# Attention with two dense layers on one core: the second layer's products 1, 5 and 2 run over gate pairs 0 to 3 before pairs 4 to 7, with a new list of places

## The chip, the cores and the metric

The kernel runs on one core of a Trainium2 chip, as one launch. The metric is the device time of that launch in microseconds. Engines are named as the profile names them: PE (matmul) with PEld (its weight loads), DVE (vector), ACT (scalar), POOL (GpSimd) and SP, which issues all DMAs here. Each engine takes its instructions in the order in which they stand in the program and waits on semaphores for the others.

## The reference

```python
def _attn_ref(q, k, v):                        # (4, 8, 576, 64) each
    ...                                        # pooled attention: means over 4 neighbours, 144 x 144, softmax
    out_up = np.repeat(out_d, 4, axis=2)
    mask = np.abs(pos[:, None] - pos[None, :]) < 4
    ...                                        # banded attention over the same q, k, v
    return out_up + out_local

x = attention, as (2304, 512)
h = x @ moe_w_in                               # (512, 2048)
x = (h / (1 + exp(-h))) @ moe_w_out            # (2048, 512)
h = x @ moe2_w_in
out = (h / (1 + exp(-1.702 * h))) @ moe2_w_out
```

The four weight matrices are float64.

## The kernel before

**Steps and places.** The kernel does not issue its work while it computes it. It adds 2663 steps to a plan (`add(name, engine, duration, function, reads, writes, buffers)`), and a string, `PLACES`, holds two characters for each step: its place in the program. `placed` reads them, checks them against the graph of dependencies, and the steps are issued in that order. So each engine's order is a table of numbers. A second table, `ON`, names the steps that run on another engine than the usual one.

**Start.** The float64 weights arrive as pairs of 32-bit words and are rebuilt in steps `ca`, `cz`, `sg`, `cs`, `cp` (ACT, DVE or POOL), then split into a high and a low fp16 half by `hi` (ACT, L376) and `lo` (DVE, L380). Each fp32 matmul of the layers is three fp16 matmuls over these halves (`TERMS`). The attention of 32 units (4 batches, 2 halves of the sequence, 4 pairs of heads) runs beside that and, from the second batch on, beside the first layer. A unit u is, in short: `KT`/`QT` (PE transposes), `SC` scores (PE), `LC`, `DM`, `LS`, `LU`, `RC`, `LN`, `PT` (DVE or POOL), `DE`, `LE`, `DN`, `TC` (ACT, some on DVE), `TP` and `AV` (PE), `UC` (ACT, L1292), `XA` (DVE, L1300). The bank that `KT` of one pair of heads writes is free again when `XA` of an earlier unit has read it.

**First layer.** Eight blocks of 288 tokens; each has 8 pairs of 128-column tiles: `h1.m.p` (PE, L702), tanh (ACT, L714), `g0` (DVE, L717), `gh` (ACT, L724), `gl` (DVE, L727), then `o1.m` (PE, L819, for block 0 L847). The PE's order among these is fixed by `chain`.

**Second layer.** Nine blocks of 256 tokens. `h_pair2(n, p)` makes gate pair p of block n: 24 matmuls into a PSUM tile (PE, L881), `th` (ACT, L893), `g0` (DVE, L896), `gs`, three additions that form the sums of Strassen's scheme (L900 to L902, on DVE or POOL as `ON` says), `gh` (ACT, L906), `gl` (DVE, L909). After the 8 pairs, `block2(n)` runs seven products of 24 matmuls each (L960) over the pairs, three matmuls per pair, into three PSUM banks `oy`, `ox` and `oz`. Of a pair's three matmuls the first two read the high half of the gate (made by `gh`), the third the low half (made by `gl`). `PARTS` lists the pieces (product, first pair, end) in PE's order:

```python
PARTS = ((1, 0, 4), (1, 4, 7), (5, 0, 4), (5, 4, 7), (2, 0, 4), (1, 7, 8), (5, 7, 8), (2, 4, 6), (6, 0, 4), ...
for prod, p0, p1 in PARTS:
    ...
    gk = [f"g{bk}.{p}" for p in range(p0, p1)]
    s = add(f"o{bk}.{prod}.{p0}", "PE", mm(3 * (p1 - p0), D2), f, r=wk + gk + [(x, "l") for x in gk], w=[bank[acc]], ...)
    chain(s)
```

Banks are read out by `e` (ACT L938, DVE L944) between products that share one. `dx`, `rm`, `am`, `pw`, `xh`, `xl` make the scales and fp16 halves of a later block's input; the PE's part of it is two matmuls (`rm`, L771).

Of the kernel before, what the change touches and what calls it, by code (L numbers as in the profile page):

```python
# [42 lines left out]


PLACES = (
    "0006020804070x030A1C0V1d2b1k050d111o2e010j0h0w0m0L0T090y1a0J1f0P1r0b0Z0M1315181l0c0U12101m1c20171L1N1P1V1U2c1I2g2r2m2y2s2C2j2M2Q2Y2Z30"
# [3 lines left out]
    "2l2x2B2p2F2I2K2L2O2R2S2W353d3n3h444w66828A2n1X2V3S2P2U2X37313c383b3k3m3u3r3v3K3H3O3X4041333f3j3y3t3D3z3J3L3P3T42464d4n4v4C4N5K43474b4i"  # L50
    "4m4o4r4y4B4H4O4R545g5h5m5w5z5C4Q4X505b5c5i5k5o5q5s5y5x5F5H5E5L5U5W5X63656A6Z768sai2G3E6148324u7s4U527B8b6f7d8o6r5R3Q3V4j5f5l5Y6n6b6s6o"
    "6x6z6B6H6F6J6T6P7e7n7t9k494c5B5N5Q6D6X6L776Y7l7v7C7M7J7N7Z7W81878c8z5T6g8j6V7w7z7P7L7U8d8f8m8n8u8r8x8H8F8K8Q8T927S7Y8O7p7x8h8B8l8D8q8v"
    "8I8L8N8R8W908X9497989b9p9u9y9Cac9FeM72858J9v8G939a9h9f9l9i9o9G9J9O9K9S9Wa9abafalbM8V8Z9w9Q9N9Z9R9Va3a5a8a7aqaCaNaOaTb1bV9maoasaAavaKaz"
    "aQaSaUaWb0b5bcaXbvbGbKbOaxaEb3b6bjb9brbtbwbybAbCbPbRbNbUbXbYbZc3c9cbchcPeoja6Q9Eag9n7XcCd3aMaFcYe9bLbxdmcHboaDbnbEb4bic0c6c5cac7cccfcg"
    "cjcmcDcOcxcVd7d9fCbqcucUbebgcycFcIcKcNcQcTcXdId6djdldLdQdUdXe3bscMdfcwczdgdqdudHdvdKdNe4e5eaedele7eCeGeIfscicldEcZd2e6egerenevexezeAeB"
    "eEeLePeDeTeXeZf0fJfNfPfTg8hXm5dceue0fbdAdCf1f4f6f9fafdfefgflfqfwfzfofYg5gcgZf8fufvfBfEfGfHfMfSfUfVfZgggjgmgEh0h3jhg0g3gfghgqgzgwgBgGgN"
    "h6gPhHhKhxhWi2i5i8gTgXh8hkhihMhmhnhPhThZi9ieihibikiuiwiMjujyjAjPjRkMjEdsfhg6gdejifgSh1gKjzitiXfRkGiWkHj4fFfKhoilioiyiDiEiLiIiJiQiRjliZ"
    "jijOk8kakgkhm1fxiVjrhrhvjejmjIjWjLjMk1k3k7ktkxkIkNl1lbldlehtjZkwj9jbkrkDkykOkPkWkYkZlWlmlwlAlYm6mdmemJl4lhlXkmkvlplGlslLlvlJlOlSlUm2mi"
    "mlmhmmmomqmLmNmVngnknMogrrjGkqlTlFkTkUmvmxmEmzmKmRmUn4njndnrnLnDnTo3odpRlulInnnsnynNnEnVnXokoqonozoKotoRoYp5qln3o7ofowouoDoEoHoJoOp6oU"
    "papopeprpPpTq9oQoTp8pbpfpkpjpqpsptpVpFpXq0q8qbqfqhqiqmqsqtqvqGquqw393w3M3Y4E4J3F3W4a4f4l4T4k4A4K4P4V4Z4F4S5d5j5p5v575e5r5G5P685t5S646l"  # L60
    "6v7k6e6k6C6G898e6t6w6I6S7G7R6O6W7f71797o7i7r7A7E7I807O7V8i868a8t8k8p8C8y8E8M8P8Y95999c9L969d9q9t9x9A9j9r9z9D9Haa9B9I9P9T9Ya19M9Ua2a6ay"
# [24 lines left out]
)
# [1435 lines left out]
```

## Time and profile before

| | us |
|---|---|
| median of 3 runs | 902.23 (901.01 to 902.79) |
| the profiled execution: its time | 902.26 |
| the profiled execution: span from first to last instruction | 900.5 |
| PE busy | 864.3 (96%) |
| DVE busy | 623.0 (69%) |
| ACT busy | 464.0 (52%) |
| POOL busy | 150.3 (17%) |

The span divides into four stretches: to 68.2 us no matmul of a layer runs; to about 150 us the first block of the first layer runs while weights are still rebuilt; to 532.9 us the other seven blocks; from there the second layer. Busy time of PE is modelled and runs from one matmul's start to its end, so a wait between two matmuls shows as an idle time in brackets in the timeline, or as a later start.

### The profile page before, as it was taken

To read this page: it belongs to the slowest core of one execution; us is meant where nothing else is said; L and a number is where in the kernel's file an instruction comes from. 1 tells how busy PE (TensorE), PEld (TensorE's weight loads), DVE (VectorE), ACT (ScalarE), POOL (GpSimd) and SP (SyncE) were. 2 spreads that over 40 slices of the span, in tenths; PEclk is the share of its full clock that TensorE was granted. 3 is DMA by queue.
4 is the path that set the end of the run, shared out by engine and by line. 5 is a ranking of instruction groups with operands and counts; after the bars stand their busy time and mean duration, and the time that the engine had idled before them with its cause. 6 is when DMAs were issued, how large, how long until landed. Compare 5 with 4: busy or idle time off the path is not lost.

```text
span 900.5 us, 23832 instructions
## 1 busy us (share of the span) xinstructions
PE 864.3 (96%) x10212; PEld 717.7 (80%) x10212; DVE 623.0 (69%) x1365; ACT 464.0 (52%) x820; POOL 150.3 (17%) x165
## 2 busy tenths in 40 slices
...
GB/s 269 204 241 230 190 63 113 69 89 127 120 118 155 150 104 98 121 106 84 129 13 293 66 41 1 12 1 24 1 25 1 36 1 13 1 36 1 25 13 36
DMA packets 116190, 77.04 MB, mean 86 GB/s; under 512 B 94836, under 2 KB 101492, under 8 KB 115060
## 3 DMA queue, kind: packets, MB, share of 16 engines
...
## 4 chain that ended last, share of the span: by engine, by line
PE 66%; DVE 25%; ACT 4%; issue 2%; DMA 2%; SPq 0%; ACTq 0%; DVEq 0%
PE hps L702 18%; PE ops L819 16%; PE oy L960 8%; DVE g L909 7%; PE hps L881 6%; PE oz L960 4%; DVE tg L896 4%; DVE tg L901 2%; PE ox L960 2%; PE ops L847 2%; DVE tg L900 2%; PE ul L1286 2%; DVE tg L902 2%; PE sl L1204 2%; DMA kraw<-in_k_dram 1%
## 5 line engine op out<-in xcount | busy, mean ns | idle before, releaser
L702 PE MATMUL hps<-xhl,win 128*128 128x288 f16 x1536 | 197.9, 288 | 0.0
L881 PE MATMUL hps<-xhl,win 128*128 128x256 f16 x1728 | 191.0, 273 | 0.2 <-DVE tg L896 0.2
L881 PEld LDWEIGHTS <-win 128*128 128x128 f16 x1728 | 168.9, 98 | 20.5 <-issue 0.6
L702 PEld LDWEIGHTS <-win 128*128 128x128 f16 x1536 | 148.9, 99 | 37.8
L819 PE MATMUL ops<-g,wout 128*128 128x288 f16 x1344 | 170.8, 287 | 0.0
L960 PEld LDWEIGHTS <-g 128*128 128x128 f16 x1512 | 146.6, 98 | 25.5 <-DVE g L909 6.5
L819 PEld LDWEIGHTS <-wout 128*128 128x128 f16 x1344 | 129.8, 98 | 32.8 <-issue 0.6
L893 ACT ACTIVATE tg<-hps,blk 128x512 f32<-128x512 f32 x72 | 49.3, 685 | 136.9 <-PE hps L881 128.8
L896 DVE SCALAR_TENSOR_TENSOR tg<-tg,hps 128x512 f32<-128x512 f32 x72 | 49.1, 682 | 54.6 <-ACT tg L893 54.6
L906 ACT ACTIVATE g<-tg 128x896 f16<-128x896 f32 x72 | 67.6, 944 | 32.1 <-DVE tg L902 30.6
L909 DVE SCALAR_TENSOR_TENSOR g<-tg,g 128x896 f16<-128x896 f32 x72 | 78.3, 1094 | 7.5 <-ACT g L906 7.2
L960 PE MATMUL oy<-wout,g 128*128 128x256 f16 x648 | 75.1, 273 | 0.3 <-DVE o L944 0.3
L714 ACT ACTIVATE tg<-hps,blk 128x576 f32<-128x576 f32 x64 | 47.1, 737 | 45.7 <-PE hps L702 37.4
L900 POOL TENSOR_TENSOR tg<-tg 128x128 f32<-128x128 f32 x9 | 6.8, 755 | 368.9 <-DVE tg L896 368.9
L717 DVE SCALAR_TENSOR_TENSOR tg<-tg,hps 128x576 f32<-128x576 f32 x64 | 47.7, 746 | 27.4 <-ACT tg L714 27.0
L348 POOL TENSOR_TENSOR cs<-cs,cz 128x512 int32<-128x512 int32 x32 | 43.0, 1346 | 134.1 <-DVE cz L336 87.6
L727 DVE SCALAR_TENSOR_TENSOR g<-tg,gs,g 128x576 f16<-128x576 f32 x56 | 47.0, 847 | 6.4 <-ACT g L724 6.3
L724 ACT ACTIVATE g<-tg,gs 128x576 f16<-128x576 f32 x56 | 42.8, 769 | 15.8 <-DVE tg L717 15.7
L938 ACT ACTIVATE o<-oy,blk 128x256 f32<-128x256 f32 x27 | 12.7, 471 | 53.8 <-PE oy L960 53.8
L323 ACT ACTIVATE st<-st 128x512 f32<-128x512 f32 (+1 forms) x48 | 39.0, 824 | 1.2 <-DMA st<-in_moe_w_out_dram 0.8
L944 DVE SCALAR_TENSOR_TENSOR o<-oy,blk,o 128x256 f32<-128x256 f32 x9 | 4.4, 484 | 47.5 <-PE oy L960 24.4
L1234 ACT ACTIVATE pd<-sl,nm 72x144 f32<-72x144 f32 x64 | 23.4, 369 | 24.1 <-DVE sc L1219 11.8
...
## 6 DMA issues: line engine op xcount, KB each, us to landing
...
```

The lines of the kernel that those rows point to most:

```text
L348: eng.tensor_tensor(out=s, in0=s, in1=zget(), op=ALU.add)
L702: nc.tensor.matmul(o, T[w][:, kc, a, fc * P:(fc + 1) * P], T[xk][:, kc, b, :T_], start=(n == 0), stop=(n == 3 * KC - 1))
L714: ACT.activation(out=T[tg], in_=T[ps][:, :, :T_], func=AF.Tanh, scale=T["a" + bk][:, c:c + 1])
L717: DVE.scalar_tensor_tensor(out=T[tg], in0=T[tg], scalar=1.0, in1=T[ps][:, :, :T_], op0=ALU.add, op1=ALU.mult)
L727: DVE.scalar_tensor_tensor(out=T[g][:, 1], in0=T[tg], scalar=gs, in1=T[g][:, 0], op0=ALU.mult, op1=ALU.subtract)
L819: nc.tensor.matmul(o, w[:, j, a, dc * P:(dc + 1) * P], g[:, b, j % 2, :], start=(n == 0), stop=(n == 3 * NF - 1))
L881: nc.tensor.matmul(o, T[w][:, kc, a, fc * P:(fc + 1) * P], T[xk][:, kc, b, :], start=(n == 0), stop=(n == 3 * KC - 1))
L893: ACT.activation(out=four(), in_=T[ps][:, 0, :], func=AF.Tanh, scale=T["a" + bk][:, c:c + 1])
L896: DVE.scalar_tensor_tensor(out=four(), in0=four(), scalar=1.0, in1=T[ps][:, 0, :], op0=ALU.add, op1=ALU.mult)
L906: ACT.activation(out=T[g][:, 0], in_=T[tg], func=AF.Copy, scale=GS2)
L909: DVE.scalar_tensor_tensor(out=T[g][:, 1], in0=T[tg], scalar=GS2, in1=T[g][:, 0], op0=ALU.mult, op1=ALU.subtract)
L960: nc.tensor.matmul(T[bank[acc]], g[:, a, slot, :], w, start=first and p == p0 and i == 0, stop=prod in (2, 3, 4) and p == NF // 2 - 1 and ...
```

## The change

Two things change. In `PARTS`, the four pairs 0 to 3 of products 1, 5 and 2 come first, then pairs 4 to 6 of products 1 and 5, then pair 7 of both; the rest of the list stands. And `PLACES` and `ON` are others: every engine's order is a new one.

```diff
 ON = {
-    "POOL": ("cp1.in.0.2 cp1.in.3.2 cp1.out.0.0 cp1.out.1.0 cp1.out.1.2 cp1.out.2.0 cp1.out.2.2 cp1.out.3.0 cp1.out.3.2"),
-    "DVE": ("sg1.in.1.2 sg1.in.2.0 sg1.out.0.0 sg1.out.1.2 LN0 LS1 LS2 LN2 LS3 LN3 LS6 LS11 LS13 LN14 LN17 LS18 LN18 LS19 "
...
-    "ACT": ("DN0 DN1 DN2 DN3 DN5 DN6 DN7 DN8 DN9 DN10 DN11 DN13 DN16 DN23 DN26"),
+    "DVE": ("sg1.in.0.0 sg1.in.0.2 sg1.in.1.2 sg1.in.3.0 sg1.out.0.2 sg1.out.1.2 LS0 LN0 LS1 LN1 LN4 LN7 LN9 LN10 LS12 LN12 "
...
+    "POOL": ("cp1.out.0.0 cp1.out.0.2 cp1.out.1.0 cp1.out.1.2 cp1.out.2.0 cp1.out.2.2 cp1.out.3.0 cp1.out.3.2"),
+    "ACT": ("DN0 DN1 DN3 DN5 DN6 DN7 DN8 DN9 DN10 DN11 DN12 DN14 DN20 DN21 DN24 DN25 DN26 DN27 DN30"),
 }
...
 PLACES = (
-    "0006020804070x030A1C0V1d2b1k050d111o2e010j0h0w0m0L0T090y1a0J1f0P1r0b0Z0M1315181l0c0U12101m1c20171L1N1P1V1U2c1I2g2r2m2y2s2C2j2M2Q2Y2Z30"
+    "0006020403070q050U1j0z1a221n0i0j0Z1v27010x080K0B0N0Y090C0R0Q110S1k0c0X0T1510181u0b0M14131A1d1B171L1Q252y2l2C1s26292j2o2r2z2f2R332Y3b36"
...
-    PARTS = ((1, 0, 4), (1, 4, 7), (5, 0, 4), (5, 4, 7), (2, 0, 4), (1, 7, 8), (5, 7, 8), (2, 4, 6), (6, 0, 4), (6, 4, 8), (3, 0, 4), (3, 4, 8),
+    PARTS = ((1, 0, 4), (5, 0, 4), (2, 0, 4), (1, 4, 7), (5, 4, 7), (1, 7, 8), (5, 7, 8), (2, 4, 6), (6, 0, 4), (6, 4, 8), (3, 0, 4), (3, 4, 8),
```

The sums `gs` that run on POOL are nine before (block 0: pairs 0, 2, 5; block 3: pairs 0, 1, 3, 4; block 4: pair 0; block 8: pair 0) and thirteen now (block 0: 0, 2, 4; blocks 1, 2 and 5: pair 0; block 3: 3, 4; block 6: 1, 2, 3, 4, 6).

**PE, the products of block 5.** The first three pieces as they stood, one row for each change of pair that matters; the number behind `g` names the pair (10825 is pair 3, 10859 pair 4, 10925 pair 6, 10960 pair 7).

```order
L960 MATMUL oy_10911<-wx_8141,g_10825 128x256
...
L960 MATMUL oy_10911<-wx_8184,g_10859 128x256
...
L960 MATMUL oy_10911<-wx_8124,g_10925 128x256
...
L960 MATMUL oz_10947<-wout2_0_8255,g_10723 128x256
...
L960 MATMUL ox_10972<-wx_7815,g_10723 128x256
...
L960 MATMUL oy_10911<-wx_8124,g_10960 128x256
```

And as they stand now (10824 is pair 3, 10858 pair 4, 10940 pair 6, 10959 pair 7).

```order
L960 MATMUL oy_10908<-wx_8111,g_10824 128x256
...
L960 MATMUL oz_10927<-wout2_0_8269,g_10723 128x256
...
L960 MATMUL ox_10945<-wx_7775,g_10723 128x256
...
L960 MATMUL oy_10908<-wx_8093,g_10858 128x256
...
L960 MATMUL oy_10908<-wx_8185,g_10940 128x256
...
L960 MATMUL oy_10908<-wx_8185,g_10959 128x256
```

Pair 4 was first used by the 13th matmul of the products and is now first used by the 37th; pair 6 by the 19th and now the 43rd; pair 7 by the 55th in both.

**DVE, the end of block 5's pairs.** From the `gl` of pair 5 on, as it stood: the `gl` of pairs 5 and 6, a read-out of the block before, `g0` and the sums of pair 7, its `gl`.

```order
L909 SCALAR_TENSOR_TENSOR g_10906<-tg_10856,g_10906 128x896
L909 SCALAR_TENSOR_TENSOR g_10925<-tg_10888,g_10925 128x896
L944 SCALAR_TENSOR_TENSOR o_10531<-ox_10509,blk_83,o_10531 128x256
L896 SCALAR_TENSOR_TENSOR tg_10927<-tg_10927,hps_10875 128x512
L900 TENSOR_TENSOR tg_10927<-tg_10927 128x128
L901 TENSOR_TENSOR tg_10927<-tg_10927 128x2x128
L902 TENSOR_TENSOR tg_10927<-tg_10927 128x128
L909 SCALAR_TENSOR_TENSOR g_10960<-tg_10927,g_10960 128x896
```

And now, from the sums of pair 6 on (tile 10889 is pair 6, 10921 pair 7):

```order
L900 TENSOR_TENSOR tg_10889<-tg_10889 128x128
L901 TENSOR_TENSOR tg_10889<-tg_10889 128x2x128
L902 TENSOR_TENSOR tg_10889<-tg_10889 128x128
L896 SCALAR_TENSOR_TENSOR tg_10921<-tg_10921,hps_10876 128x512
L900 TENSOR_TENSOR tg_10921<-tg_10921 128x128
L901 TENSOR_TENSOR tg_10921<-tg_10921 128x2x128
L902 TENSOR_TENSOR tg_10921<-tg_10921 128x128
L909 SCALAR_TENSOR_TENSOR g_10940<-tg_10889,g_10940 128x896
L283 TENSOR_SCALAR blk_83<-blk_83 128x1
L284 TENSOR_SCALAR blk_83<-blk_83 128x1
L285 RECIPROCAL blk_83<-blk_83 128x1
L909 SCALAR_TENSOR_TENSOR g_10959<-tg_10921,g_10959 128x896
```

The `g0` and the sums of pair 7 moved ahead of the `gl` of pair 6, which stands between them and the `gl` of pair 7.

**ACT, in the start.** Around the read-out `us` of unit 0 (L1292) and the scaling of unit 1's probabilities (L1251, `DN1`), as it stood:

```order
L1251 ACTIVATE pd_352<-pd_352,smr1_165 72x144 x2
L323 ACTIVATE st2_210<-st2_210 128x1024
L327 ACTIVATE z_400<-st2_212 128x1024
L344 ACTIVATE z_366<-st2_210 128x1024
L1292 ACTIVATE us_448<-ul0_403 128x288
L327 ACTIVATE z_450<-st2_195 128x1024
L344 ACTIVATE z_450<-st2_195 128x1024
L1132 COPY kT2_150<-kps_475 128x576
```

And now:

```order
L327 ACTIVATE z_383<-st2_212 128x1024
L323 ACTIVATE st2_212<-st2_212 128x1024
L344 ACTIVATE z_383<-st2_212 128x1024
L327 ACTIVATE z_433<-st2_210 128x1024
L1292 ACTIVATE us_449<-ul0_401 128x288
L376 ACTIVATE win1_0_454<-x2_80,bin1_88 128x2x512
L1251 ACTIVATE pd_356<-pd_356,smr1_165 72x144 x2
L1267 COPY pdT_504<-tps_483 72x288
```

`DN1` moved from four steps ahead of unit 0's read-out to two steps behind it, with a weight's `hi` (L376) in between. On PE the transposes of unit 1 (`TP1`), which read `DN1`'s result, still stand directly ahead of the key transposes of unit 2 (`KT0.2`).

## Rows read from the trace of the kernel before

**Rows 1.** Three stretches: length, busy time and count by engine, clock, DMA

```profile
core 0: us, PE busy (x) PEld busy (x) DVE busy (x) ACT busy (x) POOL busy (x), PEclk, DMA share, GB/s
0.00:68.20 68.20, 45.45 (x684) 41.01 (x685) 45.70 (x98) 45.47 (x78) 18.41 (x36) 1.00 0.99 237
68.20:150.00 81.80, 77.08 (x1274) 59.13 (x1275) 78.07 (x200) 67.50 (x125) 36.11 (x30) 0.96 0.59 148
...
575.00:900.50 325.50, 318.93 (x2890) 281.15 (x2887) 190.36 (x370) 120.92 (x168) 11.45 (x18) 1.00 0.04 16
```

**Rows 2.** Chain of waits, second layer: start, length, what

```profile
572.47 2.70 PE oy L960 x24
575.17 5.25 PE hps L881 x48
...
654.97 15.73 PE hps L881 x144
...
695.87 5.25 PE hps L881 x48
...
896.92 0.47 ACT o L938
```

**Rows 3.** Timeline of PE, block 5: start, length, instruction, [idle before <-releaser]

```profile
756.53 2.35 PE L960 MATMUL oy<-wx,g 128*128 128x256 f16 x20
759.20 0.28 PE L960 MATMUL oy<-wx,g 128*128 128x256 f16 x1 [0.32 <-DVE g L909]
```

**Rows 4.** Timeline of DVE and ACT, block 5, pairs 5 to 7

```profile
756.95 2.19 DVE L909 SCALAR_TENSOR_TENSOR g<-tg,g 128x896 f16<-128x896 f32 x2
757.92 0.67 ACT L893 ACTIVATE tg<-hps,blk 128x512 f32<-128x512 f32 x1
...
759.46 0.68 DVE L896 SCALAR_TENSOR_TENSOR tg<-tg,hps 128x512 f32<-128x512 f32 x1
...
761.28 0.95 ACT L906 ACTIVATE g<-tg 128x896 f16<-128x896 f32 x1 [1.65 <-DVE tg L902]
...
762.26 1.09 DVE L909 SCALAR_TENSOR_TENSOR g<-tg,g 128x896 f16<-128x896 f32 x1 [1.02 <-ACT g L906]
```

**Rows 5.** Timeline of PE, end of block 0

```profile
557.48 0.28 PE L960 MATMUL oy<-wx,g 128*128 128x256 f16 x1 [0.41 <-DVE g L909]
...
560.85 0.49 PE L771 MATMUL rm<-dgx,ones 128*128 128x128 f32 x2 [0.79 <-DVE dgx L764]
```

**Rows 6.** Timeline of the start, all engines

```profile
19.48 0.64 ACT L1132 COPY kT<-kps 128x576 f32<-128x576 f32 x1 [1.75 <-PE kps L1129]
...
25.87 0.71 ACT L1251 ACTIVATE pd<-pd,smr 72x144 f32<-72x144 f32 x2
...
27.50 1.14 ACT L327 ACTIVATE z<-st 128x1024 int32<-128x1024 uint32 x1
28.53 1.34 ACT L344 ACTIVATE z<-st 128x1024 f16<-128x1024 f32 x1
...
31.58 0.37 PE L1128 MATMUL kps<-ident,kraw 96*128 96x96 f32 x1
...
32.13 1.21 DVE L348 CUSTOM_DVE_ANT_0 x<-x,z 128x2048 uint16<-128x2048 uint16 x1
...
32.61 2.94 POOL L348 TENSOR_TENSOR x<-x,z 128x1024 int32<-128x1024 int32 x1 [3.77 <-ACT z L344]
...
33.26 2.90 DVE L336 TENSOR_SCALAR z<-st 128x1024 uint16<-128x1024 uint16 x1
...
70.25 0.75 DVE L336 TENSOR_SCALAR z<-st 128x1024 uint16<-128x1024 uint16 x1
```

**Rows 7.** Timeline of block 3: sums on POOL beside DVE

```profile
659.16 0.45 POOL L900 TENSOR_TENSOR tg<-tg 128x128 f32<-128x128 f32 x1 [105.36 <-DVE tg L896]
...
667.58 2.35 DVE L909 SCALAR_TENSOR_TENSOR g<-tg,g 128x896 f16<-128x896 f32 x2
667.64 1.35 POOL L900 TENSOR_TENSOR tg<-tg 128x128 f32<-128x128 f32 x1 [4.05 <-DVE tg L896]
```

More of the change, by code (lines that the diff above doesn't have):

```diff
@@ L50 @@
[L50 to L61, printed above, removed]
@@ new lines @@
+    "3e2F3g3r3o3v3u3J0V0W1b1r1q211i1p1y1F1Z2c2v2x2G2M2L2W3E3G3V47414S2B372Z3i3m3k3z4d2I3I4a3O4u4e4p4H3K4K4P5054535k5f3F4v4F4D5s5E5I5Q4I5H5O"
+    "64636a6m6I4x5a5B5Z5V686l6d5w6R6e6W7f727b7t5W6M7B6U7H74797O4q4w6h6q6n6t5N676x7170756z7e7j7n7p7D7c7k7L7Z7Y828P0a0e0f0d0g0h0n0l0p0o0r0t0u"
+    "0v0A0D0G0F12191c1e0m0s160k0w0y0I0E0L0H0J0O0P1h1f1l1o1x1C1H1J1W1m1t1S1g1w1z1D1E1G1I1K1M1O1R1P1X231U2g2n2q2t1N1V2p1T1Y202a282e2b2d2h2i2m"
+    "2k2u2w2s2A2E2H2J2N2Q2S2X34302V3j3H4W6b7r8p242D2O3M2K2P2T38313d393f3l3n3A3q3s3B3C3L3Q3U3X323c3p3x3t3D3y3N3R3T44464b4i4c4t4C4J4N3Y45484k"
@@ new lines @@
+    "4h4m4o4E4L4X5751555g5e5o5u5A5F4M4T4V56595j5c5i5p5q5v5x5D5G5z5L5T5X6265666Z787h8SbJ2U356k423h4A6T4R4Z5K7N5M6D8f5Y7G3Z4G3W5l5m616o6g6s6p"
+    "6u6y6B6G6E6H6V6N7i7m7v9C4l5h5y5C5S6w6Q6K737a7A7C7I7M7S7W837P858a8d9E5U6c877y7z7F7V7R808e8i8o8q8D8t8y8A8G8N8U9194888c8v8h8k8n8x8w8E8F8K"
+    "8M8Q8V8W969a9b9e9j9k9l9K9P9Ua4acaMfV8u8l98ab95979m9t9r9B9y9A9G9H9J9N9Qad9Makarayc78Y8Z9La79Vaa9Za1agaoauaqaGaJb0b7b9bbcp9RataBaHaWb4aZ"
+    "b1bcbebGbnbwbzbIbNbTbUbWawaCbhbobmbAbCbFbMbPbZbQbXc0c1c3c5c6c9cvcycGcJdidGjh8C9fazas9haVddaLaibpdzbLa3cKcFbB9qbyaDb2bKc8cdcbciccceclcm"
@@ new lines @@
+    "cqcnctcxcscZdkdneA9Ya2bibsbvcocQcucTcMcPcWcXd0dgdAdEdBdVe0e2e8aQbScBchcSdsdFdDdIdHdTdWe9edeaefeyeleCeIeKfqbucLd4cYe4ebenegeqeieoetevez"
+    "eFeMePeOeSeUeWeYftfEfGfTg5fJfKd5d1fQffdRe6eZf1f2f5f7faflfofNfwfHfLfRfYg7gaghexfsfufyfBfOfMfXg0g3grg6gmgpgBgEgJgLgYgdggglgngqgsgugygPgQ"
+    "gUgWh4hahDhMhQhThWfAgRhchvhihChthEhHhRhUi0i1i3hYi6icifigiWj2j6j8jxjmpubtdNg4gMdtgDiNgFgch6jLiIfFjHkikliSfPfUgvhshNihioiniripiDiFiKjbiR"
+    "jdjsjnjBjDjGjJfDgegZhlhyiOjgj7jjjajNjPjSjUjVk3k8jWkskykDm6jqjuiiiUiXjRkck9kgkdknkpkCkXkGkLlslglzlDlHm9hnialIjfkrkIlalcltlhlulwlxlElJlQ"
@@ new lines @@
+    "lTlZm0m2m3m8mamNmRnknpntqAjTjAl2lLkPkRmdmjmkmnmmmAmGmImLmOn8ncn6nAnHnUo2kMmomyn0mDnon7nbnsnunxnznYo0omoDoJoLqbmumKo9ogoeoloiotoyoAoFoG"
+    "oOp1oHp9prptpMmFoPoVoYp2oZp4p7pcphpoplpwpDpBpJpPpRq8qdqgqiqqqVqFqk3a3w3S434s4B3P40494f4j4r4g4n4z4Q4U524y4O4Y5b5r5J585d5n5P696C5t5R606i"
+    "6X7g6f6j6v6F7u7K6r6A6J6O7w846L6P776Y767o7d7l7s7q7x7T7J7Q867X818m898g8s8r8z8T8H8R929c9d9w90999g9n9o9W9i9p9u9z9Ia99s9x9F9O9Saj9D9Ta0a6af"
+    "aA9Xa5ahamaOaSa8aeanaFaKbgapaxaEaNaRbfaIaPaXb5b6d2aUb3bjbDc2dpb8bdbkbrbxbEbRbYcDc4cacfcjcwcEcHcOcVcUd3d7d9dedOd6dbdjdodrdLdhdmdxdye1ec"
@@ new lines @@
+    "dwdCdSdUe7esdJdQdXdYeQeRdZe5eeejemepehekeueBeEfcereweXf6fzgCeHeNeTf0f4fbfhfjg9fnfxfCfIfSg2g8gfgkgjgogwgzgXh5gtgxgGgHgKgNgIgOgVh0h2h8gS"
+    "h1h9hbhfhhh7hghkhrhFhJhjhqhxhAhIhLhwhBhKhOhVjQhGhPi4i5iekehXi2i9imiqiviAiJjziLiQiYj4j9jejljtjIjCjKjYjZk1k2jXk0k4k7kbkzk5kakjkokqkAkfkm"
+    "ktkwkWl3kvkBkFkHkJkQkEkNkTkZlblekSl1l5l7lolql4l8lflklmlPldljlnlrlvlClMlRmglYm1m5mimlmqmvmCmJmHmQmTmVn4nwmSmWn3ndngnnn2n9njnlnBnMninmny"
+    "nCnKnQnqnvnDnJoqownFnLnTnWohosnSnZo5o8pzpGo4odozoCoKqpojoroxoIoQoXp0p5pvpfpkpppspypFpOpTpXpWpZq2q4q7qyq3q6qfqlqoqrqeqmqtquqxqCqsqvqEqH"
@@ new lines @@
+    "r1r4qDqJqQqTrardqRqWqYr0r3rhqXr2r8rbrerUr6rcrjrzrCrRrkrorurArFrIrOrTsarWrXrZs4s8sfsismspsosssvswszsAsusxsCsDsFsLsBsEsHsJsUsYsGsKsPsQsT"
+    "t4sOsRsXt0t3t5sVt1t7t9tbtft6tatetitmtptstutxtwtAtCtEtGtItLtPtX6S7U8b8I8L8Xal937E8B8j8J9vavcgbVaTblbHbqbOcrdacA8OckbacNcIdueJdKaYd8czdf"
+    "dcdlfgdqcCdveVeLf3f9fdfecRdPe3fWeDfZh3gidMeGfifkfmfrfvg1f8gAgbhehmhphzhugThZhdi8i7idilikfpiyiuiBiEiHiViMhohSijisitixiZiCibiziTj5j3jcjO"
+    "jyiGj0iPjkjijpjvjwiwjEjrkhjMkkl9kujFkOk6kVkUl0lplSjokKl6lilylBlWlFkxlOlVm4lXm7mrmekYlGlNmblUmxmUmElAmpmcmtmsmwmPnhmhmBmXmYmZn1nXn5mfmM"
```

42 lines of the change are left out of this document (15 added, 27 removed), and 10 rows, old and new, of the table ON.

## The prediction
> **What bounds the kernel now.** I read the windows by stretch first, then the chain of waits for the second layer, then the timeline around one block's products, and last the start. The windows show three regimes [rows 1]. Up to 68.2 us PE is busy 45.45 us and DMA runs at 0.99: no layer's matmul can start before weights and the first four units are done. From 68.2 to 150 us DVE is busy 78.07 of 81.80 us and sets the pace, and the granted clock of 0.96 says that PE falls to its lower level, 1.2 GHz, for a part of it. From 150 us on PE hardly stands still, and what is left are small waits. A wait that goes there is worth its full length, since everything behind it moves up; time lost in the start is lost to the end for the same reason.
>
> **The second layer, blocks 1 to 8.** The chain gives the starts of the blocks [rows 2]: the first matmuls of block 1 begin at 575.17, the last read-out at 896.92, so eight blocks take 321.75 us. A matmul that waits for nothing takes 15.73/144 = 0.1092 us, and a block has 192 + 168 = 360 of them, 39.32 us; eight are 314.6 us. The excess is 7.2 us. Four of the blocks hold a pair of `rm` matmuls, 0.2 us each (a pair takes 0.49 us to its modelled end [rows 5], of which a part lies over the next matmul; 0.9 in all), and the last product waits for the read-out of its bank for about 0.1 us per block (2.70 us [rows 2] where 24 matmuls take 24 x 0.1092 = 2.62; 0.8 in all). Neither changes. About 5.5 us remain, and they are waits for `gl`.
>
> Block 5 shows them [rows 3, 4]. The products start at 756.53. Of the three matmuls of a pair only the third reads the low half, which `gl` makes. For pair 6 in product 1 that is the 21st, due 20 x 0.109 = 2.18 us later, at 758.71; its `gl` is the second of the two that end at 756.95 + 2.19 = 759.14, and PE starts again at 759.20. That loses 0.5 us. Then pair 7: its low half is read by the 57th matmul, due 56 x 0.109 = 6.1 us behind the start, and 0.5 for the loss, at 763.1; its `gl` ends at 762.26 + 1.09 = 763.35, 0.3 more lost. Block 5 loses 0.8 us.
>
> The trap is plain in these rows. The new order of the products alone would make pair 6's low half due by the 45th matmul, at 756.53 + 44 x 0.109 = 761.3, and the first loss would go; but pair 7's stays at the 57th, due at 762.6, and its `gl` at 763.35 would then hold PE for 0.8 us, as much as both losses together. The products alone gain nothing. What decides is DVE's order. In it the `gl` of pair 6 (1.09) now stands behind the `g0` and the sums of pair 7, whose tanh is ready at 757.92 + 0.67 = 758.59, and DVE idled 1.02 us ahead of the last `gl` while ACT made the high half [rows 4]. With 1.09 us of work put into that idle time, the last `gl` ends about 1.0 earlier: 762.35. In this block three tiny scale steps stand there too, but the read-out that stood ahead of pair 7 (between 759.14 and 759.46) has gone from the stretch, which is about as much. Due 762.6, ready 762.35: no wait, with 0.3 to spare. Pair 6's `gl` ends one `gl` and the scale steps earlier, about 760.8, due 761.3.
>
> So the wait falls from 0.8 to about 0 in this block. Blocks 4 and 7 have no extra step on DVE in that stretch, blocks 1, 2 and 5 send the sums of pair 0 to POOL, block 2 has a reduction of a later block in it, block 6 two scale steps ahead of its last `gl`, block 8 a read-out. Since the margin is some 0.3 us, I leave 0.2 us of wait per block, 1.6 in all. **Term: 5.5 - 1.6 = 3.9 us gained**, between 1.0 (the margin missed by 0.55 us in each block) and 5.5 (none left).
>
> **Block 0.** There DVE still splits the last weights while it makes the pairs. PE loses 0.41 for pair 6 and 0.79 for `rm` behind a `dx` [rows 5], and the last `gl` comes only just in time behind them. Now that `rm` stands in a later block and one `rm` ahead of the last pair; but the list of DVE up to the last `gl` is as long as before (one `lo` of 1.28 moved between the sums and the `gl` of pair 7, where it fills the wait). So PE mostly trades these waits for one at pair 7. **Term: 0.4 us gained**, between 0 and 1.2.
>
> **The start.** It is all new, and nothing in it is on the subject of the products. By the two tables, DVE takes over two rebuilding steps `cp` of 1.21 from POOL and gives one back, and takes over, net, two `sg` of 0.75 from ACT and a few short attention steps (0.5 in all, an estimate from their size): some 3.2 us more [rows 6]. ACT is relieved of two `sg` of 1.34 and one scaling of 0.71: 3.4 less. POOL has one `cp` less. Against that stands a collision that goes: the `cp` on POOL from 32.61 (2.94 us) beside which DVE's `sg` took 2.90 instead of 0.75, 2.15 lost [rows 6]; this `cp` is now on DVE. And three DVE steps of later units stand now behind the last weight half rather than ahead of it, about 1.2. With that, DVE's list up to the last step that the first block's last products wait for is about as long as it was (3.2 more, 2.15 and 1.2 less). **Term: 0**, between 3.4 gained (ACT's relief wholly on the path) and 3.2 lost (DVE's extra steps wholly on it). I take 0 as what the list's length gives.
>
> **The first layer from 150 us** has the same matmuls in nearly the same order, and PE waits there for almost nothing; attention's small matmuls are cut in at other places, but as often. Term 0, with 0.5 to either side.
>
> Sum on the profiled execution's own 902.26 us (span 900.5; the median of the runs is 902.23, so nothing is to be corrected): 902.26 - 3.9 - 0.4 = 898.0 us.
>
> **Rivals.**
>
> *The waits move to pair 7.* If ACT holds the high half of pair 7 back, because it makes pair 6's first (0.95 each, now back to back behind a tanh), the last `gl` stays where it was and each block loses at its 57th matmul what it lost before. Then only some tenths in all are gained: 902.26 - 0.8 = 901.5. For it: due and ready lie 0.3 apart in the walk. Against it: the high half of pair 6 can start as soon as its sums end, 1.7 us before those of pair 7 end, and takes 0.95.
>
> *POOL's sums hold up DVE.* Thirteen sums on POOL instead of nine, five of them in block 6. In block 3, with four, the period was 695.87 - 654.97 = 40.90 us against 40.1 for the mean of the other seven [rows 2], 0.8 more. Beside a pair of `gl` on DVE (2.35 where 2.19 is usual) an addition on POOL took 1.35 instead of 0.45 [rows 7]. Block 6, where pair 6's sums are on POOL too and ACT's queue puts pair 7's high half behind pair 6's, would lose 1.5 (0.8 scaled by five to four, and 0.5 for pair 6), block 3 0.8 as before: 898.0 + 2.3 = 900.3. Against it: block 6 has 4 us less on DVE. The Trainium skill has this as a rule: in "SBUF — State Buffer", section "Who interferes with whom", a DVE instruction with two SBUF inputs and a GpSimd instruction that reads SBUF shut each other out, and the later one waits for the whole of the earlier. The trace agrees: 0.9 us on POOL, 0.16 on DVE in these rows.
>
> *The start comes later; this ends slower.* The place is PE's `KT0.2` at 31.58 [rows 6]. It stands behind `TP1`, which needs `DN1` (0.71 on ACT, at 25.87 before). Between the key copies, which end near 20.3, and the end of `DN1` ACT now has seven conversions and one `hi`, all eight of 1.14's shape, one `sg` of 1.34, two scalings of 0.71 and five small steps, taken at 0.5: 9.1 + 1.3 + 1.4 + 2.5 = 14.3 us. So `DN1` ends at 34.6 instead of 26.6 and `KT0.2` starts near 35.1, 3.5 later. If unit 3 meets the same, the first layer starts 7.0 later than 68.2, and nothing behind takes that up: 898.0 + 7.0 = 905.0. It decides from 6.1 us on. Against it: unit 1's read-out, which `KT0.3` waits for, depends on ACT steps that moved ahead, and by my walk it comes back to 43 us, where it was.
>
> *It does not do what it says*: a dependency pins the places around the products. The rows of the new order show the moves, so little is left for it: no change, 902.
>
> **Chances.** The forecast 0.61, its own range 895 to 900; POOL's sums 0.12; the waits at pair 7 0.13; the late start 0.11; no change 0.03. A change under 0.2% (1.8 us) is what a measurement here can't tell from none. Faster by more than that: 0.61 and 0.11 of POOL's case, 0.72. Within it: 0.13 + 0.03 and the other 0.01 of POOL's case, 0.17. Slower: 0.11. The range runs from 894.2 (5.5 and 1.2 gained in the second layer, 1.4 of ACT's relief) to 902.4, which takes in the waits at pair 7 and leaves out the late start.
>
> **What would show it.** In the profile after: blocks 1 to 8 take some 39.6 to 39.9 us each in the chain of waits; PE's idle time ahead of L960 for `gl` falls from about 5.5 to under 2 us; DVE's last `gl` of a block follows another `gl` with no idle time; block 6 is the longest. The first L702 matmul lies within 66 to 70 us. The forecast is wrong if the last `gl` still ends later than 6.1 us behind the first product in most blocks, or if that first matmul moves by more than 3 us.

## The result, and the profile after

| | median, us | runs | ratio to before |
|---|---|---|---|
| before, beside it | 901.62 | 900.22 to 902.79 | |
| after | 909.86 | 909.14 to 910.95 | 1.0093 [1.0073, 1.0113] |

The change made the kernel 0.9% slower; 898.0 was predicted, with a range to 902.4. The profiled execution took 909.14 us (span 907.4), 6.9 more than the one of before.

First the windows, cut at the same events as [rows 1]: up to the first product of the first layer, then block 0 of that layer, then blocks 1 to 8 of the second layer.

```profile
0.00:68.30 68.30, 45.71 (x684) 40.87 (x685) 42.31 (x100) 42.12 (x73) 16.50 (x37) 1.00 0.89 225
68.30:159.90 91.60, 79.63 (x1206) 59.96 (x1205) 87.10 (x188) 69.67 (x123) 37.82 (x27) 0.91 0.64 142
...
585.90:907.40 321.50, 317.08 (x2892) 282.51 (x2890) 191.22 (x372) 121.36 (x168) 20.16 (x30) 1.00 0.04 16
```

Block 0 of the first layer in the kernel before:

```profile
68.20:148.50 80.30, 75.58 (x1261) 57.92 (x1261) 76.99 (x195) 66.48 (x122) 34.69 (x28) 0.96 0.59 150
```

The first stretch ends at 68.3 us, as it did. Block 0 of the first layer, which ran from 68.2 to 148.5 before (80.3 us), now takes 91.6. In it DVE is busy 87.10 us with fewer instructions than before (188; before 195 in 76.99 us): about the same work, but longer. PE's granted clock fell from 0.96 to 0.91. In these two traces all of the loss is there; by the first matmuls of the stages it grows from 0.1 us at 68 us to 11.4 at the end of block 0, and is still 11.5 at the start of the second layer.

The second layer did what was forecast. The chain of waits ends with these rows (start, length, what), and PE's timeline gives the start of block 1:

```profile
824.89 20.96 PE hps L881 x192
...
864.27 20.96 PE hps L881 x192
...
903.75 0.47 ACT o L938
```

```profile
585.92 2.35 PE L881 MATMUL hps<-xhl,win 128*128 128x256 f16 x20
```

And the same matmul in the kernel before:

```profile
575.00 3.22 PE L881 MATMUL hps<-xhl,win 128*128 128x256 f16 x28
```

Block 7 takes 864.27 - 824.89 = 39.38 us, nearly the wait-free 39.32 of the prediction. Blocks 1 to 8 take 903.75 - 585.92 = 317.83, and before, from the same matmul in PE's timeline, 896.92 [rows 2] - 575.00 = 321.92: 4.1 us gained. Block 0 takes 41.5 against 42.1.

What PE waited for in blocks 1 to 8 (us in all, times, longest), first now, then the waits for `gl` before:

```profile
PE rm L771 <- DVE dgx L764: 0.5, 1, 0.5
PE oy L960 <- DVE g L909: 0.3, 1, 0.3
```

```profile
PE oy L960 <- DVE g L909: 1.8, 5, 0.6
```

These are the waits that show as idle time; those that show as a later start are not in them.

Block 5 in the timelines of PE and DVE, to be held against [rows 3, 4]:

```profile
766.09 1.47 PE L960 MATMUL oy<-wx,g 128*128 128x256 f16 x12
...
770.02 1.15 PE L960 MATMUL oy<-wx,g 128*128 128x256 f16 x9
...
771.98 0.49 PE L960 MATMUL oy<-wx,g 128*128 128x256 f16 x3
```

```profile
769.15 1.08 DVE L909 SCALAR_TENSOR_TENSOR g<-tg,g 128x896 f16<-128x896 f32 x1
...
770.60 1.07 DVE L909 SCALAR_TENSOR_TENSOR g<-tg,g 128x896 f16<-128x896 f32 x1
```

No brackets are left: pair 6's `gl` ends at 770.23 and the last one at 771.67, 5.6 us behind the first product, while the 57th matmul is due at 6.1.

Where the loss is made shows at two places of block 0 of the first layer. DVE, POOL and PE near 107 us (start, length, instruction, [idle before <-releaser]):

```profile
107.36 0.29 DVE L575 TENSOR_REDUCE sum_out<-spo 128x1 f32<-128x128 f32 x1 [0.21 <-PE spo L572]
107.57 2.82 DVE L727 SCALAR_TENSOR_TENSOR g<-tg,g 128x576 f16<-128x576 f32 x1
...
107.41 2.37 POOL L348 TENSOR_TENSOR x<-x,z 128x1024 int32<-128x1024 int32 x1 [2.69 <-PE spo L572]
...
108.82 3.06 PE L702 MATMUL hps<-xhl,win 128*128 128x288 f16 x12
112.69 0.76 PE L1198 MATMUL sl<-kd,qd 64*72 64x144 f32 x4 [0.81 <-DVE xf L1301]
```

and near 140 us:

```profile
140.19 2.32 DVE L1245 TENSOR_SCALAR smr<-smr 128x8 f32<-128x8 f32 x1
...
142.66 1.66 DVE L727 SCALAR_TENSOR_TENSOR g<-tg,g 128x576 f16<-128x576 f32 x1
...
139.28 3.20 POOL L348 TENSOR_TENSOR x<-x,z 128x1024 int32<-128x1024 int32 x1 [3.89 <-DMA qraw<-in_q_dram]
142.44 1.27 POOL L1148 TENSOR_TENSOR vraw<-vraw 72x512 f32<-72x512 f32 x1
...
146.94 1.43 PE L847 MATMUL ops<-g,wout 128*128 128x288 f16 x8 [3.06 <-DVE x L861]
```

At 107.57 a `gl` (L727, usually 0.75) begins 0.16 us behind a POOL sum (`cp`, L348) and goes on until 0.6 us behind the sum's end. At 140.19 an instruction of 8 columns, 0.17 elsewhere, takes 2.32, again to the end of the sum. There is no bracket: a standstill counts as busy, which is why DVE's busy time rose. PE then waits for what stands behind it on DVE, 0.81 for `XA7` and 3.06 for the read-out L861. In the kernel before, the same sum (`cp1.out.1.2`) ran beside other instructions:

```profile
102.72 0.47 DVE L1183 STREAM_TRANSPOSE qT<-qraw 128x288 f32<-128x288 f32 x1
103.22 0.45 DVE L1187 TENSOR_REDUCE qd<-qT 128x72 f32<-128x288 f32 x1
103.59 0.77 DVE L1137 STREAM_TRANSPOSE kT<-kraw 128x576 f32<-128x576 f32 x1
104.28 0.33 DVE L1300 TENSOR_TENSOR xf<-ul,us 128x72 f32<-128x72 f32 x2
...
102.60 2.36 POOL L348 TENSOR_TENSOR x<-x,z 128x1024 int32<-128x1024 int32 x1
```

None of these is longer than usual. Both kernels run eight such sums in block 0; what differs is what stands beside them. Taken over block 0, with the median of each line and shape in the trace of before as its usual length, DVE's instructions that run over 0.1 us too long lose 4.2 us before (7 instructions) and 13.3 after (12): 9.1 of the 11.3 us by which the block grew.

### The profile page after: what moved, and what is told of

Read it like the earlier page. It is cut to its first block, busy times and chain, and to the rows that moved or that the text cites. A ratio compares the mean times of both kernels' runs of the same rounds, so it can differ in the third digit from the quotient of the medians.

```text
span 907.4 us, 23876 instructions
## 1 busy us (share of the span) xinstructions
PE 867.4 (96%) x10212; PEld 722.2 (80%) x10212; DVE 627.1 (69%) x1354; ACT 467.8 (52%) x826; POOL 158.6 (17%) x174
## 5 line engine op out<-in xcount | busy, mean ns | idle before, releaser
L702 PE MATMUL hps<-xhl,win 128*128 128x288 f16 x1536 | 200.1, 289 | 0.3 <-DVE xhl L786 0.3
L702 PEld LDWEIGHTS <-win 128*128 128x128 f16 x1536 | 149.5, 99 | 38.8 <-issue 0.6
L960 PEld LDWEIGHTS <-g 128*128 128x128 f16 x1512 | 147.5, 98 | 20.1 <-DVE g L909 1.5
L960 PE MATMUL oy<-wout,g 128*128 128x256 f16 x648 | 75.1, 272 | 0.0
L348 POOL TENSOR_TENSOR cs<-cs,cz 128x512 int32<-128x512 int32 x32 | 43.3, 1356 | 113.8 <-DVE cz L336 42.9
L900 POOL TENSOR_TENSOR tg<-tg 128x128 f32<-128x128 f32 x13 | 10.8, 830 | 294.7 <-DVE tg L896 294.6
L727 DVE SCALAR_TENSOR_TENSOR g<-tg,gs,g 128x576 f16<-128x576 f32 x56 | 50.5, 915 | 4.5 <-ACT g L724 4.4
L1228 POOL TENSOR_TENSOR sc<-sc,mx 128x192 f32<-128x192 f32 x21 | 15.5, 739 | 105.1 <-DVE mx L1222 105.1
```

What stands on the lines that cost most here:

```text
L348: eng.tensor_tensor(out=s, in0=s, in1=zget(), op=ALU.add)
L702: nc.tensor.matmul(o, T[w][:, kc, a, fc * P:(fc + 1) * P], T[xk][:, kc, b, :T_], start=(n == 0), stop=(n == 3 * KC - 1))
L727: DVE.scalar_tensor_tensor(out=T[g][:, 1], in0=T[tg], scalar=gs, in1=T[g][:, 0], op0=ALU.mult, op1=ALU.subtract)
L960: nc.tensor.matmul(T[bank[acc]], g[:, a, slot, :], w, start=first and p == p0 and i == 0, stop=prod in (2, 3, 4) and p == NF // 2 - 1 and ...
```

## The experiments

The theory after the result (called S and L in the expectations): the second layer's gain is real, and the loss is made in block 0 of the first layer, where VectorE (DVE) instructions stand still beside POOL's sums. Each run has its own executions of the kernel before beside it (901.04 to 901.19). The last two columns are the first matmuls of block 1 of the first layer and of the second layer in the trace, which is of one execution: e3's took 901.40 us and f3's 903.74, some way from their medians.

| run | median, us | ratio, 95% | block 1 | layer 2 |
|---|---|---|---|---|
| before | | | 148.5 | 532.9 |
| after | 909.86 | [1.0073, 1.0113] | 159.9 | 544.4 |
| e1_layer2_alone | 897.44 | [0.9947, 0.9973] | 146.5 | 531.4 |
| e2_start_alone | 917.79 | [1.0169, 1.0199] | 159.0 | 549.0 |
| e3_first68_alone | 903.47 | [1.0014, 1.0033] | 148.0 | 532.3 |
| e4_after_from68 | 907.33 | [1.0046, 1.0080] | 158.1 | 542.7 |
| f1_after_short_sums | 893.96 | [0.9906, 0.9948] | 144.9 | 529.4 |
| f2_before_short_sums | 898.59 | [0.9961, 0.9982] | 143.8 | 528.3 |
| f3_after_reordered | 900.62 | [0.9983, 1.0006] | 154.5 | 539.0 |
| f4_layer2_and_repair | 897.41 | [0.9942, 0.9970] | 148.3 | 533.2 |
| g1_after_sums_in_four | 900.10 | [0.9984, 1.0003] | 150.2 | 534.7 |
| g2_layer2_sums_in_four | 896.86 | [0.9937, 0.9967] | 147.7 | 532.1 |
| e5_products_alone | 901.28 | [0.9993, 1.0012] | 147.2 | 531.6 |
| g3_before_two_placed | 904.13 | [1.0021, 1.0047] | 149.9 | 534.5 |

### Which stretch loses

Four kernels are spliced from the two tables of places and engines: up to a named step from one kernel, the rest from the other.

```diff
 PLACES, ON, PARTS
+e1: before up to h2.0.0.0 (second layer), then after
+e2: after up to h1.2.0.0 (third block of the first layer), then before
+e3: after up to h1.0.0.0 (68 us), then before
+e4: before up to h1.0.0.0, then after
```

> Places and engines of the kernel before for every step up to the first product of the second layer's block 0; from there on those of the changed kernel, with its order of products. Theory S (the second layer gained what the prediction said, and the loss lies wholly in the places that were searched anew for the start): 901.6 - 4.7 = about 897 us, first matmul of the second layer at 533 us as before, blocks 1 to 8 some 4.1 us shorter together. Rival W (the changed second layer costs something as a whole, and the gain by blocks is only that everything in it comes 11 us later, after its loads): 901 to 904 us.

> The mirror image up to the third block of the first layer: places and engines of the changed kernel up to the first product of block 2 of the first layer (at some 176 us), from there on those of the kernel before, with its order of products. Theory S: 901.6 + 12 = about 913 to 914 us, the second matmul stretch of block 0 (product of pair 3 in the second tile of o1.0) at some 158 us against 146 before. Rival W (no loss of its own in the start): 901 to 903 us.

> Places and engines of the changed kernel only up to the first product of the first layer's block 0 (68 us in both traces), from there on those of the kernel before. Theory S1 (the loss is made by the order of the instructions behind 68 us, and the first 68 us cost nothing, since that product starts at 68.2 and 68.3 us in the two traces): 901 to 903 us. Rival S0 (the first 68 us leave VectorE or the loads further behind, which shows only later): 906 to 914 us.

> The kernel before up to the first product of the first layer's block 0, from there on the changed kernel to its end. Theory S1: the changed kernel's loss and gain are both there, about 909 us. Rival S0: the loss is gone and the second layer's gain is left, about 897 us; values between would share the loss out over the two stretches.

e1 came out at 897.4, where S put it: the new second layer alone is worth 3.6 us of 901.04 (2.4 to 4.8 by the interval). e2 is slower by 16.7, more than expected; 4.5 us of it appear between blocks 2 and 3 of the first layer, just behind the splice, so they belong to the seam and not to the start. e4 is 9.9 us above e1, from which it differs only between 68 us and the second layer. e3 is between: 2.2 us (1.3 to 3.0) slower in the medians, though its profiled execution, at 901.40 us 2.1 below e3's median, begins block 1 half a microsecond earlier than before. So some 10 of the 12 us that part the changed kernel from e1 are made by the order behind 68 us, and about 2 ahead of it; those 2 are not explained, and that trace can hardly show them.

### What loses there: the sums on POOL

f1 and f2 cut the sums in the two kernels to 64 of 1024 columns, and leave the rest of those rebuilt weights out:

```diff
             s = r().bitcast(I32)
-            eng.tensor_tensor(out=s, in0=s, in1=zget(), op=ALU.add)
+            z1 = zget()
+            if eng is POOL and L.n == 1:
+                s, z1 = s[:, :64], z1[:, :64]
+            eng.tensor_tensor(out=s, in0=s, in1=z1, op=ALU.add)
```

> The changed kernel, with each of POOL's eight integer sums of the first layer's weights (the tensor_tensor of L348, 2.4 us each) done on 64 of 1024 columns only: that part of the rebuilt weights is left out. All orders and engines stay. Theory L (lock: some VectorE instructions stand still until a POOL instruction beside them ends; in the changed kernel five of them stand directly behind the start of a sum, 7.9 us over their usual lengths in VectorE between 82 and 142 us, and the PE waits 1.4 to 3.2 us behind them): those instructions return to 0.2 to 1.3 us, and the kernel to 900 to 903 us. Rival O (the order itself: the instructions that free PSUM for PE stand too far back in VectorE's list): PE's waits stay, 908 to 910 us.

> The same cut in the kernel before. Theory L: only two instructions stand still beside a sum there (1.98 and 1.19 us for some 0.15 us), 2.8 us of VectorE in all, so at most 3 us less than before: 898 to 900 us. If what the changed kernel's cut brings came from rebuilt weights that are ready earlier, and not from the lock, this kernel would gain as much, 893 to 895 us.

f1, same order and same engines, came to 893.96, below the forecast of its own theory; by the two ratios to before (1.0093 and 0.9927) that is 15 us less than the changed kernel. Its DVE and POOL at the place shown above (line numbers from L348 on are three higher here), and its window of block 0:

```profile
101.52 0.32 POOL L351 TENSOR_TENSOR x<-x,z 128x64 int32<-128x64 int32 x1 [2.55 <-PE spo L575]
...
102.08 0.75 DVE L730 SCALAR_TENSOR_TENSOR g<-tg,g 128x576 f16<-128x576 f32 x1
```

```profile
67.90:144.90 77.00, 72.83 (x1207) 56.09 (x1206) 74.18 (x188) 68.61 (x124) 19.05 (x27) 1.00 0.75 165
```

The `gl` is back at 0.75; block 0 takes 77.0 us, and the same 188 instructions of DVE 74.18 in place of 87.10. Four instructions still run too long, by 1.0 us in all. The rival O, that the order itself loses, falls: the order is unchanged, and its block is faster than the one before. The theory had counted five instructions beside a sum. But 12.3 us of the 13.3 went, since POOL's other sums (L1148, L1149), no longer held up in its queue, stopped meeting DVE as well. f2 gained only 2.6 us, with standstills down from 4.2 to 1.3, which speaks against rebuilt weights that are ready sooner as the source of f1's gain.

The clock is the second part. Two windows of the changed kernel, then the same of f1, then of f3 (below):

```profile
95.00:105.00 10.00, 8.90 (x168) 6.74 (x166) 9.76 (x20) 8.43 (x19) 5.57 (x5) 1.00 0.57 152
105.00:115.00 10.00, 7.96 (x139) 5.74 (x140) 9.22 (x23) 8.12 (x10) 2.37 (x1) 0.59 1.02 218
```

```profile
95.00:105.00 10.00, 9.13 (x172) 6.87 (x169) 9.76 (x30) 9.72 (x19) 3.06 (x5) 1.00 0.88 212
105.00:115.00 10.00, 9.25 (x170) 7.13 (x171) 9.79 (x27) 9.26 (x16) 1.95 (x4) 1.00 1.12 186
```

```profile
95.00:105.00 10.00, 8.20 (x124) 6.30 (x123) 8.78 (x25) 8.02 (x17) 6.15 (x6) 0.96 0.67 168
105.00:115.00 10.00, 10.00 (x146) 7.25 (x144) 7.79 (x25) 8.72 (x11) 4.15 (x3) 0.53 0.97 209
```

In the changed kernel and in f3's profiled execution the granted clock is 0.59 and 0.53 from 105 to 115 us, mostly the lower level of 1.2 GHz, behind stretches in which PE had waited (busy 8.90 and 8.20 of 10); the 12 matmuls at 108.82 took 3.06 us there, and the same 12 in f1 1.65. In f1, busy 9.13, the clock stayed at 1.00. For the changed kernel that is usual, with a mean clock over the execution of 0.988 to 0.992 in all four; for f3 it is not: the profiled one had 0.992, its other nine 0.996 to 0.999.

How much of f1's 15 us is clock and how much standstill no run parts, but e1 allows an estimate. Its instructions in block 0 are those of the kernel before, and that block took 78.8 us at a clock of 1.00 there against 80.3 at 0.96. At that rate a clock of 0.91 over 91.6 us costs about 4 us; the other 11 would be left to the standstills.

### Moving DVE's instructions, with the sums left whole

f3 alters DVE's order in block 0 of the changed kernel; f4 does the like in e1.

```diff
 DVE, f3
-so1.0 gl1.0.1 sg1.out.0.2 so1.0p gl1.0.0 cs1.out.1.2 KD1.0 XA5 LU6 XM5 g01.0.2
+so1.0 gl1.0.1 so1.0p gl1.0.0 sg1.out.0.2 KD1.0 XA5 LU6 XM5 g01.0.2 cs1.out.1.2
-LU7 RC7 sg1.out.1.2 LN7 PT7 XA6 QX9 XM6 spm1.out.1.2 gl1.0.3 so1.1 g01.0.4 QD9 KX1.2 XA7
+LU7 XA6 QX9 XM6 RC7 sg1.out.1.2 LN7 PT7 spm1.out.1.2 so1.1 g01.0.4 QD9 KX1.2 XA7 gl1.0.3
...
-XA8 QX10 QD10 LU9 lo1.out.2.2 RC9 gl1.0.6 LN9 PT9 LC10 ev1.0.1.1 DM10
+XA8 QX10 lo1.out.2.2 QD10 LU9 RC9 LN9 PT9 ev1.0.1.1 LC10 DM10 gl1.0.6
 DVE, f4
-so1.3 gl1.0.5 so1.3p QX11 XA8 LU9 QD10 QD11 ev1.0.1.0 RC9 lo1.out.2.0 lo1.out.2.2 LC10 DM10
+so1.3 so1.3p QX11 XA8 LU9 QD10 QD11 ev1.0.1.0 gl1.0.5 RC9 lo1.out.2.0 DM10 lo1.out.2.2 LC10
```

> The changed kernel with VectorE's order altered at four places of block 0 of the first layer, nothing else: so1.0p, gl1.0.3, so1.3p, RC7 and RC9 (with what hangs on them) no longer stand directly behind the start of a POOL sum; instructions that read PSUM or reduce one operand stand there. POOL's sums keep their whole length. Theory L: the moved instructions fall from 2.2 to 2.8 us to their usual lengths, PE's waits for XA5, XA6 and ev1.0.1.1 (1.9, 2.1, 3.2 us) go, 901 to 905 us. Rival X (any order lets some instruction stand behind a sum, VectorE has no others to put there): other instructions of 2 us and more, 907 to 911 us.

> The kernel of the first run (start and first layer of before, second layer of the changed one, 897.4 us) with VectorE's order altered at one place of block 0 of the first layer: so1.3p stands ahead of gl1.0.5, DM10 ahead of the second lo. Theory L: so1.3p falls from 2.44 to 0.6 us, DM10 from 1.63 to 0.6, PE's wait of 2.0 us ahead of SC10 goes: 894.5 to 896 us. If VectorE's standstills were not on the path there: 897 to 898 us.

f3 regained 9 us by the ratios: 900.62, just below the 901 to 905 of L. Standstills fell from 13.3 to 5.9 us, but, as the rival X said, another instruction took a place beside a sum:

```profile
129.14 3.54 DVE L786 SCALAR_TENSOR_TENSOR xhl<-xf,blk,xhl 128x1152 f16<-128x1152 f32 x1
```

1.41 is usual for it. f4 missed: 897.41, no gain over e1. The two instructions that were moved took 0.6 us each, but the next `gl` now stood behind the second sum and waited instead (lines one lower here: L726 is `gl`, L347 the sum):

```profile
130.84 2.26 DVE L726 SCALAR_TENSOR_TENSOR g<-tg,g 128x576 f16<-128x576 f32 x1
...
129.60 2.88 POOL L347 TENSOR_TENSOR x<-x,z 128x1024 int32<-128x1024 int32 x1 [0.73 <-ACT z L343]
```

Its time is the one that was named for standstills that are not on the path. By the count above they fell from 4.2 us in e1 to 2.6, so what they cost at this place stays open.

### Shorter sums, all work kept

```diff
-            s = r().bitcast(I32)
-            eng.tensor_tensor(out=s, in0=s, in1=zget(), op=ALU.add)
+            s, z1, w = r().bitcast(I32), zget(), 256 if eng is POOL and L.n == 1 else N
+            [eng.tensor_tensor(out=s[:, a:a + w], in0=s[:, a:a + w], in1=z1[:, a:a + w], op=ALU.add) for a in range(0, N, w)]
```

> The changed kernel with each of POOL's eight integer sums of the first layer (2.4 us) written as four instructions of 256 columns, all work kept. Theory L: a VectorE instruction that stands still waits for one POOL instruction only, so at most some 0.7 us in place of 2.3: the five standstills fall from 7.9 us to 2 or 3, and with them the low-clock stretch of 105 to 115 us; 897 to 902 us. Rival M (a VectorE instruction waits for POOL's whole run of work, since POOL's next instruction is let in first): standstills as long as before, and POOL longer by its fixed part, 909 to 912 us.

> The kernel of the first run (start of before, second layer of the changed one, 897.4 us) with the sums in four in the same way. Theory L: the two standstills of 1.98 and 1.19 us shrink, 894 to 897 us. Rival M: 898 to 900 us.

g1 regained 9 us by the ratios, with no step moved. Its DVE and POOL beside two of the sums:

```profile
128.36 1.82 DVE L380 SCALAR_TENSOR_TENSOR wout<-x,bout,wout 128x1024 f16<-128x1024 f32 x1
...
133.77 0.70 DVE L1245 TENSOR_SCALAR smr<-smr 128x8 f32<-128x8 f32 x1
...
125.73 5.03 POOL L348 TENSOR_TENSOR x<-x,z 128x256 int32<-128x256 int32 x4 [3.93 <-ACT z L344]
133.25 3.08 POOL L348 TENSOR_TENSOR x<-x,z 128x256 int32<-128x256 int32 x3 [2.48 <-ACT z L344]
```

L1245, 2.32 in the changed kernel, takes 0.70: it waits for one quarter (the last row shows three of that sum's four). And the four pieces at 125.73, 0.73 each when alone, take 5.03 us, since POOL in turn waits for DVE's instructions between them. By the count above 7.1 us of standstill are left, in 17 shorter pieces. The rival M, that DVE waits for POOL's whole run of work, falls. g2 is 0.6 us below e1, which their intervals don't tell apart.

### The products alone, and the reverse test

```diff
 e5, second layer, PE only
-o2.n: 1.0 1.4 5.0 5.4 2.0 1.7 5.7
+o2.n: 1.0 5.0 2.0 1.4 5.4 1.7 5.7
 g3, DVE of the kernel before
-gl1.0.3 XA6 XM6 PT7 g01.0.4 spm1.out.1.2 XM5 so1.1 QX9
+XA6 XM6 PT7 g01.0.4 spm1.out.1.2 XM5 so1.1 QX9 gl1.0.3
-lo1.out.2.0 lo1.out.2.2 LC10
+lo1.out.2.0 LC10 lo1.out.2.2
```

> The kernel before with nothing changed but the order of products in the second layer on PE (products 1, 5, 2 over pairs 0 to 3, then 1 and 5 over pairs 4 to 6, then pair 7); every other engine keeps the order of before. Theory of the prediction (the gain of 4.1 us of blocks 1 to 8 needs the gate of pair 6 ahead in the DVE and ACT orders too, or the wait only moves to pair 6 or 7): part of it, 899 to 902 us. Rival (the order of products is all of it): 896.5 to 898 us.

> The reverse test, on the kernel before: two instructions of VectorE that read two operands from SBUF are put behind the start of a POOL sum: gl1.0.3 from ahead of XA6 to behind QX9 (inside the sum of 102.6 to 104.95 us), lo1.out.2.2 from ahead of LC10 to behind it (inside the sum of 130.6 us). All else stays. Theory L: gl1.0.3 takes 2 to 2.4 us for 0.71, the second lo 2.5 to 3.3 us for 1.5, what follows them is later, 903 to 905 us. Rival O (a place in VectorE's list without a lock costs nothing here): 900.5 to 902 us.

e5 gained nothing: 901.28 against 901.06. Block 5 on PE:

```profile
757.47 1.47 PE L960 MATMUL ox<-wx,g 128*128 128x256 f16 x12 [0.27 <-DVE o L944]
...
761.29 0.28 PE L960 MATMUL oy<-wx,g 128*128 128x256 f16 x1 [0.17 <-DVE g L909]
```

and what PE's L960 waited for from 573 us to 900, in all (us, times, longest):

```profile
PE oz L960 <- DVE o L944: 1.4, 1, 1.4
PE oy L960 <- DVE g L909: 1.2, 4, 0.7
PE ox L960 <- DVE o L944: 0.8, 3, 0.3
PE oy L960 <- DVE o L944: 0.4, 1, 0.4
```

In the kernel before the same view has 1.8 us for `gl` and 0.3 for a read-out. Some of the wait stays at `gl`, the rest moves to DVE's read-outs (L944) of banks that are now wanted earlier. So the gain needs the other engines' new orders in the second layer as well; by the rows of block 5 it is DVE's, but no run changes DVE's alone.

g3 made the kernel before 3.1 us slower by two moved instructions. The one stood still as meant; the other did not, since the sum began later, at 132.04, but `DM10`'s scaling (L1214, usually 0.17) did, for 1.83 us in place of the 1.19 of the kernel before:

```profile
101.66 2.25 DVE L727 SCALAR_TENSOR_TENSOR g<-tg,g 128x576 f16<-128x576 f32 x1
...
133.35 1.83 DVE L1214 TENSOR_SCALAR nm<-nm 72x2 f32<-72x2 f32 x1
...
100.93 2.36 POOL L348 TENSOR_TENSOR x<-x,z 128x1024 int32<-128x1024 int32 x1
...
132.04 3.13 POOL L348 TENSOR_TENSOR x<-x,z 128x1024 int32<-128x1024 int32 x1 [0.56 <-ACT z L344]
```

## Why the prediction was wrong, step by step

**Blocks 1 to 8, term 3.9.** Right in size and mechanism: 4.1 us in the traces (the prediction's 321.75 begins 0.17 later, where the chain of waits has block 1's first matmul). The waits for `gl` are nearly gone, and DVE idles ahead of a `gl` once, for 0.4 us (before 8 times, 6.8 us). That the products alone gain nothing is shown by e5, though the walk had all of the wait at pair 7, and much of it came at DVE's read-outs. Wrong in a detail: block 3, not 6, is the longest (40.6 us), in part by a wait of 0.5 us ahead of `rm`; block 6, with five sums on POOL, took 40.2.

**Block 0, term 0.4.** 0.6 in the trace. e1 confirms the two terms together in the medians: 3.6 us against 4.3, which lies within its interval.

**The first layer from 150 us, term 0.** Within the half microsecond: 11.4 us late at the end of its block 0, 11.5 at the second layer.

**The start, term 0.** This step failed: "DVE's list up to the last step that the first block's last products wait for is about as long as it was", and "I take 0 as what the list's length gives." The list is as long: by usual lengths DVE's instructions up to block 1 add up to 128.6 us before and 129.3 now. The time to run it is not, and the term came out at 11.4 us lost. The prediction counted one meeting of a POOL sum with DVE, the 2.15 us at 32.61 that goes [rows 6], and none of those that come behind 68 us. There 13.3 us of standstill stand against 4.2. f1 shows the sums to be the cause, f3 and g1 that moving what stands beside them, or making them shorter, gives 9 us back, g3 that the like moves cost the kernel before 3.1 us, and e4 that the place is behind 68 us. A part of the loss came by way of the lower clock, on which the prediction set no price: by the estimate above about 4 us now, against 1.5 in the trace of before. The bound of 3.2 us lost counted the added steps as the worst that DVE could meet, and no new meeting with a sum.

The rule was in hand. The rival of POOL's sums used it for the thirteen small sums of the second layer (0.45 us an addition) and not for the eight of 2.4 us in block 0 of the first. The Trainium skill, "SBUF — State Buffer", section "Who interferes with whom", also says which instructions are free of it: those with at most one SBUF input outside the two-port modes, and on this chip every `tensor_reduce`; `tensor_scalar` can enter such a mode when its operands meet the conditions. The rows agree: beside a sum `TENSOR_REDUCE` took its 0.45 and the two of `XA`, one input of which lies in PSUM, their 0.33, while `gl` and the 8-column `TENSOR_SCALAR` stood for 2.82 and 2.32.

**The late start.** `KT0.2` moved to 36.30 (35.1 by the walk, 31.58 before), `KT0.3` to 45.2 (43 by the walk, 43.78 before), and the first product stood at 68.3. That rival was rightly put aside. But the sign that was named for the start, the first L702 matmul, lay ahead of the stretch that lost, so it read "right" while the kernel lost 11 us behind it.

**The best of both.** The start of before with the new second layer (e1, 897.4, and with the sums in four 896.9) beats the kernel before by 0.4% to 0.5%, and the changed one by more.
